# The first pair's blocks go to the inverse and back by VectorE transpositions, with a new list of the first 640 steps

## The chip, the cores and the metric

One core of one Trainium2 chip runs the whole kernel. The metric is the device time of one execution in microseconds (us), lower is better. A profile of one execution stands beside the timed runs: its span runs from the first instruction to the last, and the execution's own time is a little longer than that span.

The engines are named as in the profile: PE (TensorE), DVE (VectorE), ACT (ScalarE), POOL (GpSimd), and SP, which here does nothing but issue DMAs. "SPq" and "ACTq" are the time that a queue takes to issue a DMA.

## The reference

Two blocks follow each other. The first is a delta rule over 768 tokens, for 4 batches and 8 heads of 48 features:

```python
k_n = k / (np.linalg.norm(k, axis=-1, keepdims=True) + 1e-06)
state = np.zeros((B, H, D, D), dtype=np.float32)
for t in range(S):
    kt, vt, bt = (k_n[:, :, t], v[:, :, t], beta[:, :, t, None])
    y[:, :, t] = np.einsum('bhd,bhde->bhe', q[:, :, t], state)
    v_old = np.einsum('bhde,bhd->bhe', state, kt)
    state = state + bt[:, :, :, None] * np.einsum('bhd,bhe->bhde', kt, vt - v_old)
```

Its output, as x of 3072 tokens by 384 features, goes through the second:

```python
a = x @ w1          # 384 x 1024
b = x @ w2          # 384 x 1024
h = a * b @ w3      # 1024 x 1024
return (h @ w_out).astype(np.float32)   # 1024 x 384
```

q, k, v and beta come as float32. The four weights come as float64, so they are twice as many bytes, and the kernel makes float32 of them itself.

## The kernel before, in words

**The delta rule in chunks.** The 768 tokens are cut into 12 chunks of 64, and two chunks m = 2j, 2j+1 make a pair j. For each chunk a lower triangular system has to be inverted, of 64 x 64 for each of 32 heads (4 batches by 8 heads). It is done on blocks of 32 x 32: the two blocks on the diagonal of each system are inverted, and `corner` makes the third block out of them by matmuls. A pair has 2 chunks x 32 heads x 2 blocks = 128 diagonal blocks, one for each partition. `inverse(j)` (L483) holds one block in each partition, 32 x 32 = 1024 numbers in its free dimension, and eliminates them on DVE in 31 steps of two instructions (a product, L503, and a subtraction, L508).

**How the blocks come there and go back, before.** The scores `first_scores` or `scores` write U with tokens on the partitions. `to_blocks(m)` (L471) writes the blocks to a DRAM buffer Ud with 4 DMAs a chunk, `inverse` reads them back with one DMA (L489) into Ub, with blocks on the partitions. It ends with one DMA (L516) to a DRAM buffer Vd, and `from_blocks(m)` (L522) reads them with 4 DMAs a chunk into TT (L525) and 4 into T22 (L532), tokens on the partitions again. For the first two pairs the elimination runs in PSUM: ACT copies the unit matrix there (L497) and the result back to Vb (L512).

**The rest of a chunk.** `by_tensor` (L359) turns keys and queries to features on the partitions with PE, `squares` and `norms` make the scales of the keys, `corner` (L539) the inverse, `chain` (L606) the state, and `outputs` (L686) the transposed output xT. Since a matmul of the second block reads 128 partitions and a half has only 112 rows, `outputs` copies some rows of xT to free partitions by 6 DMAs a chunk (L748).

**The weights.** A piece of float64 is loaded by `piece` (L759) into one of 5 tiles named raw, which are used in turn, and made to float32 in three further steps: two ACT instructions, one of DVE (L776), one of POOL (L778). There are 36 pieces, P0 to P35: 8 of w_out, 16 of w3, 6 of w1, 6 of w2; a piece of w1 or w2 takes 4 DMAs, the others one. w3 is transposed on PE (`transpose_w3`, L828) and multiplied with w_out once (`fold`, L837: 8 folds of 8 matmuls), so that each token later goes through w3 @ w_out in one product.

**The second block.** `ab(u, jc, c0, c1)` (L851) makes a * b for 128 of the 1024 features and the tokens of a pair of chunks. For the first pair it is done for each chunk alone (256 tokens in a matmul, steps b0 to b7 and a00 to a07), for the next ones for both (512). `slab_sums`, `o` (L1067) and `result` make the output products with seven instead of eight block products (Strassen's scheme). The last pair takes `features` instead of `ab`.

**The order.** Nothing is scheduled when the kernel runs. ORDER is a list of 1379 step names that stands in the file; each name starts a generator or moves it to its next `yield`, and each engine and each DMA queue works off its own instructions strictly in that text order. So an instruction that waits holds up all behind it on its engine. Step names: k, q, v load a chunk; K, Q turn it; g, N are squares and norms; s and h are scores (in the first pair the keys' and the queries'), u writes blocks to DRAM, V is the inverse, e the corner, c the chain, y the outputs, P a piece, t and f the transposition of w3 and the fold, b and a the products of the second block, S, o, x its output, p and d the keys and queries by DMA and DVE from the fifth chunk on.

## Time and profile before

| | us |
|---|---|
| three timed runs | 575.88, 576.21, 573.61 (median 575.88) |
| the profiled execution | 575.02 |
| its span | 573.3 |
| PE busy | 537.3 (94%) |
| DVE busy | 336.7 (59%) |
| POOL busy | 173.1 (30%) |
| ACT busy | 143.6 (25%) |
| moved by DMA | 56.57 MB, mean 99 GB/s |

The page shows the busy share of each engine in 40 slices of 14.3 us each, then the chain of work that ended last, the costliest groups of instructions, and the DMA issues. The groups and the timeline count each float32 matmul twice, since PE runs it as two instructions: "x64" in a row of PE are 32 matmuls of the code. A row of the timeline gives the start, the duration, the engine, the line and the operation, the number of merged instructions, and in brackets the idle time ahead of it with what ended it. A row of the view by stretches gives, for each stretch, the busy time and the number of instructions of each engine, the granted PE clock (1.00 is full), the busy share of the DMA engines, and the rate in GB/s.

### The profile page before, as it was taken

Reading aid. Unit: us, or ns where it says so; the run is one execution under the profiler, and the core shown is the slowest. Engines: PE = TensorE matmul, PEld = TensorE weight load, DVE = VectorE, ACT = ScalarE, POOL = GpSimd, SP = SyncE. Lnnn points to the kernel's source line nnn. Section 1 sums busy time; section 2 is a strip of 40 time slices with the busy share of each in tenths; the row PEclk is TensorE's granted clock in tenths of the full one; section 3 lists DMA queues with packets and bytes.
Section 4 is the critical chain, followed back from the end, with each engine's and each line's share of the span. In section 5 each row is a group of like instructions: output and inputs, shape, how many; then the busy total and the mean of one; then the engine's idle time right before and its main releaser. Section 6 shows DMA issues by size and latency. Waiting matters only on the chain.

```text
span 573.3 us, 19695 instructions
## 1 busy us (share of the span) xinstructions
PE 537.3 (94%) x8588; PEld 393.3 (69%) x8588; DVE 336.7 (59%) x795; ACT 143.6 (25%) x289; POOL 173.1 (30%) x217
## 2 busy tenths in 40 slices
PE   2889888899999999998999999999999999989997
PEld 1765556688889744597644699444986446988897
DVE  4739823449854659765795735696264974123552
ACT  4466545624112110130120120110310102212210
POOL 6565543212883000524121332002731006610000
PEclk9979999999999999999999999999999999999999
DMA  9888997459746371564446425733325113010001
GB/s 218 233 242 229 216 198 148 90 128 173 126 74 111 61 137 32 110 98 84 92 75 110 63 47 105 125 65 82 42 46 125 20 51 58 18 53 5 0 1 55
DMA packets 202806, 56.57 MB, mean 99 GB/s; under 512 B 189952, under 2 KB 196096, under 8 KB 202720
## 3 DMA queue, kind: packets, MB, share of 16 engines
q1 hardware_dynamic: 200608, 54.92, 47.8%
q8 instruction: 67, 1.10, 0.8%
q10 hardware_dynamic: 2112, 0.39, 0.4%
q14 instruction: 19, 0.16, 0.1%
HBM read 43.09 MB, written 11.01 MB: 94 GB/s over the span
## 4 chain that ended last, share of the span: by engine, by line
PE 66%; DVE 11%; DMA 11%; SPq 4%; ACT 3%; issue 3%; POOL 2%; ACTq 0%; DVEq 0%; POOLq 0%
PE ps_f L858 26%; PE ps_f L1090 19%; PE ps_w L614 4%; PE ps_f L998 4%; DVE tb L503 4%; PE ps_w L719 4%; DMA raw<-in_moe_w_dram 4%; PE ps_w L998 2%; DVE ps_w L508 2%; PE ps_w L561 2%; DMA ktok<-in_k_dram 2%; DVE Vb L508 2%; DMA Vd<-Vb 2%; PE ps_w L437 1%; SPq L763 1%
## 5 line engine op out<-in xcount | busy, mean ns | idle before, releaser
L858 PE MATMUL ps_f<-xT,w2s 128*128 128x512 f32 (+1 forms) x288 | 107.1, 525 | 0.6 <-DVE ab L874 0.4
L858 PE MATMUL ps_f<-xT,w1s 128*128 128x512 f32 (+1 forms) x288 | 105.9, 524 | 0.3 <-DMA xT<-xT 0.3
L858 PEld LDWEIGHTS ps_f<-xT,w2s 128*128 128x128 f32 x288 | 53.9, 190 | 46.3 <-issue 41.3
L858 PEld LDWEIGHTS ps_f<-xT,w1s 128*128 128x128 f32 x288 | 54.1, 190 | 45.6 <-issue 42.5
L931 POOL TENSOR_TENSOR ab<-ab 128x256 f32<-128x256 f32 x80 | 56.0, 725 | 40.8 <-DVE ab L874 29.3
L1090 PE MATMUL ps_f<-w,ab 128*128 128x192 f32 x320 | 56.8, 331 | 2.0 <-DVE osb L1119 1.3
L1090 PEld LDWEIGHTS ps_f<-w,ab 128*128 128x128 f32 x320 | 51.6, 190 | 3.6 <-issue 2.8
L870 ACT COPY ab<-ps_f 128x512 f32<-128x512 f32 (+1 forms) x48 | 23.3, 515 | 121.5 <-PE ps_f L858 117.9
L503 DVE TENSOR_TENSOR tb<-Vb,Ub 128x31 f32<-128x31 f32 (+15 forms) x124 | 43.6, 352 | 15.8 <-DMA Ub<-Ud 12.1
L508 DVE TENSOR_TENSOR Vb<-Vb,tb 128x31 f32<-128x31 f32 (+15 forms) x124 | 45.1, 364 | 4.3
L837 PE MATMUL ps_f<-wo,w3T 128*128 128x384 f32 x128 | 44.9, 500 | 2.9 <-ACT w3T L831 1.9
L1090 PE MATMUL ps_f<-room,ab 128*128 128x192 f32 x240 | 43.2, 332 | 0.1
L299 POOL TENSOR_TENSOR sq<-ktok 128x384 f32<-128x384 f32 x24 | 20.3, 849 | 67.7 <-DMA ktok<-in_k_dram 39.0
L1090 PEld LDWEIGHTS ps_f<-room,ab 128*128 128x128 f32 x240 | 38.6, 190 | 1.2 <-issue 0.4
L837 PEld LDWEIGHTS ps_f<-wo,w3T 128*128 128x128 f32 x128 | 23.8, 194 | 18.6 <-ACT w3T L831 2.7
L874 DVE TENSOR_TENSOR ab<-ab,ps_f 128x512 f32<-128x512 f32 (+1 forms) x48 | 27.4, 589 | 13.3 <-PE ps_f L858 13.3
L600 POOL TENSOR_TENSOR vtok<-vtok,n 128x384 f32<-128x384 f32 x24 | 20.3, 850 | 45.3 <-DMA vtok<-in_v_dram 32.9
L577 ACT COPY T<-ps_w 32x512 f32<-32x512 f32 x24 | 13.8, 575 | 77.7 <-PE ps_w L561 67.2
L737 ACT COPY xT<-ps_w 112x256 f32<-112x256 f32 x48 | 14.3, 384 | 65.7 <-PE ps_w L719 65.7
L778 POOL TENSOR_TENSOR w<-w,raw 128x512 uint32<-128x512 uint32 x16 | 21.2, 1330 | 18.1 <-DVE w L776 14.3
L437 PE MATMUL ps_w<-KQ 48*64 48x128 f32 x320 | 21.8, 275 | 3.2 <-DVE PT L460 1.4
L503 DVE TENSOR_TENSOR tb<-ps_w,Ub 128x31 f32<-128x31 f32 (+15 forms) x62 | 21.0, 338 | 4.0 <-ACT ps_w L497 2.6
(148 smaller groups left out, 780.8 us busy)
## 6 DMA issues: line engine op xcount, KB each, us to landing
raw<-in_moe_w_dram SPq DMA_DIRECT2D x16, 512.0 KB, 5.6
vtok<-in_v_dram SPq DMA_DIRECT2D x24, 192.0 KB, 4.6
raw<-in_moe_w_dram SPq DMA_DIRECT2D x24, 192.0 KB, 5.0
out_dram<-osb SPq DMA_DIRECT2D x46, 96.0 KB, 1.8
ktok<-in_k_dram SPq DMA_DIRECT2D x44, 96.0 KB, 3.6
raw<-in_moe_w_out_dram SPq DMA_DIRECT2D x8, 384.0 KB, 5.1
Ud<-U SPq DMA_DIRECT2D x48, 64.0 KB, 2.0
Ub<-Ud SPq DMA_DIRECT2D x6, 512.0 KB, 3.9
```

What stands on the lines that cost most here:

```text
L437: pe.matmul(ps[half(z), 0, n : n + 128], lhsT=x[:, 0, :], rhs=x.rearrange("p j t -> p (j t)"), start=True, stop=True,)
L503: dve.tensor_tensor(out=tv, in0=V[:, 0 : s + 1, s : s + 1].to_broadcast([P, s + 1, n]), in1=U[:, s, s + 1 : BS].unsqueeze(1).to_broadcast( ...
L508: dve.tensor_tensor(out=o, in0=o, in1=tv, op=ALU.subtract)
L614: pe.matmul(out(ps, r, h, z), lhsT=lhs(r, h, z), rhs=rhs(r, h, z), start=True, stop=True,)
L719: i = pe.matmul(region(h, z, r), lhsT=lhs, rhs=rhs, start=part[n] not in part[:n], stop=part[n] not in part[n + 1 :],)
L837: pe.matmul(ps[:, 0:DM], lhsT=w3Ts[jc, kc // 4][:, kc % 4 * P : kc % 4 * P + P], rhs=wo(kc), start=(kc == 0), stop=(kc == KF - 1),)
L858: pe.matmul(ps[:].rearrange("p b c t -> p b (c t)"), lhsT=w[:, m, js], rhs=x[:, m, :, c0:c1].rearrange("p b c t -> p b (c t)"), start=(m = ...
L870: act.copy(out=t, in_=ps)
L874: dve.tensor_tensor(out=t, in0=t, in1=ps, op=ALU.mult)
L931: (dve if u == last else pool).tensor_tensor(out=o_, in0=x_, in1=y_, op=op)
L998: pe.matmul(ps[:, j, :], lhsT=w[j], rhs=x, start=first and j == 0, stop=j == 1, skip_group_check=not first,)
L1090: pe.matmul(ps[b][:, b, :], lhsT=ab_of(u, HF * f + i, t0), rhs=ws_[w][:, i], start=first and i == 0 and (b == 0 or n == "F"), stop=i == HF ...
```

## The change

Only the first pair (chunks 0 and 1, inverse 0) takes a new way; the other five pairs go through DRAM as before.

- **Into the inverse.** The two U tiles become one tile Upair, so that one DVE transposition reads both chunks. DVE transposes blocks of 32 x 32, so within each quarter of 32 partitions the (chunk, head) of a block becomes the partition, and token row and column lie in the free dimension. For that the block of the second token half has to lie in the columns of the first as well, so `keys_or_queries` makes the keys' scores with two matmuls of 32 rows each in place of one of 64 rows, and the second of them writes its block twice. `to_blocks` is not called for m = 0 and 1 (8 DMAs less), nor the load of Ub (1 less).
- **Out of the inverse.** Four transpositions, each of one quarter of 32 partitions and 1024 numbers, read the result in PSUM and write TT. The two ACT copies to Vb, the DMA to Vd, and 16 DMAs of `from_blocks` are not done. T22 is made by `from_engines`: 4 PE matmuls with the unit matrix and 2 ACT copies a chunk.
- **DMAs on the ACT queue.** Of the keys of chunks 0 and 1, two of four DMAs each are issued by ACT (before: all four of chunk 0 by ACT, all four of chunk 1 by SP). Of the 6 DMAs of xT of chunks 0 and 1, ACT issues 3.
- **More tiles for pieces.** 12 of the 36 pieces are loaded not into a raw tile but into kperm, qperm, or one of two parts of a tile of the KQ ring, all of which are unused at that time. kperm and qperm are no longer set to zero at the start.
- **The list.** The first 667 names of ORDER are replaced by 670 others; the last 712 are the same.

```diff
@@ ORDER
-k0 P12 beta P3 P3 g0 P8 g0 P8 P0 g0 P12 K0 K0 k1 P12 P13 P12 K1 K0 q1 P3 beta P0 g0 P0 P10 P8 g0
...
+k0 P12 g0 k1 K0 P2 P8 P12 beta K1 g0 P8 P13 g0 K0 P1 g0 g0 V0 P2 P8 P10 K1 P5 P2 K0 P12 g0 beta s0
...
+P26 t8 V0 f5 P27 P35 t6 t14 P20 t6 q2 V0 P24 k3 P15 P15 f4 V0 V0 h0 f4 v0 t15 f4 t7 e0 Q2 e0 P20
+e0 t7 e0 Q2 P20 P21 f3 e0 K2 g1 e1 e0 g1 v1 q3 P27 f3 n0 P26 P32 P24 e0 P20 e1 P35 K1 P21 e1 e1
+P28 K2 n0 P35 c0 Q2 P24 f7 c0 e1 P28 g1 f7 g1 e1 P27 P21 P27 P33 K2 P21 f3 f7 c0 c0 K0 P29 e1 t12
+P25 t13 P32 n1 c1 t13 t12 K3 g1 P29 K3 K3 y0 P34 k4 g1 y0 f6 Q3 y0 P29 n1 c1 P33 P29 y0 c1 P24 c1
+P33 f6 y1 P34 b5 Q3 P25 Q3 N1 y1 f6 s3 P34 P25 P31 s2 s3 P30 s2 y1 b4 P31 y1 P30 s3 s3 b5 s3 P34
+P33 b6 P25 b2 u3 s2 s2 a07 P30 s2 b4 b6 P32 b3 a07 u2 V1 P31 s3 v2 P30 b4 g2 b2 b5 a07 V1 s2 V1 b3
+b0 b4 g2 b6 a07 n2 b5 V1 P31 a04 b0 a00 V1 v3 a06 b6 g2 V1 c1 a04 a00 b1 V1 V1 a01 V1 b1 V1 V1 a06
+T V1 V1 V1 a02 b7 V1 P32 T a01 V1 a02 V1 a03 n3 a03 V1 V1 p4 b7 V1 a04 T V1 Q3 n3 V1 a00 a01 V1 V1
+a05 a04 n2 V1 a05 a00 V1 V1 a01 p4 a03 V1 b0 a03 a02 k5 b1 b2 V1 V1 V1 b0 V1 V1 S0 V1 g2 a02 b3 d4
+b1 V1 g2 T V1 g2 b3 b2 b7 V1 d4 a05 a05 g2 a06 c1 b7 g2 o0 S0 g2 c2 a06 e2 S0 S0 e2 x0 e2 c2 e3 N1
+o0 e2 e2 d4 S0 e2 V2 S0 p5 g2 o0 c2 e3 d4 Q0 S0 p5 x0 N1 S0 c2 e3 x0 o0 e3 S0 e3 c2 e3 N2 c2 S0 c3
+S0 S0 S0 o0 c3 x0 y2 y2 v4 d5 c3 o0 n4 c3 y3 d5 v5 s4 S0 d5 y3 d5 x0 S0 x0 s4 s4 x0 s5 S0 y3 s4 x0
...
@@ load_crossed
-                dma(
+                dmas[z](
@@ keys_or_queries
+                    if j:
+                        pe.matmul(
+                            ps[half(z ^ h % 2), h % 2, n : n + C],
+                            lhsT=x[:, 0, :], rhs=x[:, 1, :], start=True, stop=True,
+                        )
+                        continue
+                    own = x[:, 0, BS:C].unsqueeze(1).to_broadcast([D, 2, BS])
+                    for y, rhs in enumerate((x[:, 0, :], own)):
+                        pe.matmul(
+                            ps[quarter(2 * z + y), h % 2, n : n + C],
+                            lhsT=x[:, 0, BS * y : BS * y + BS], rhs=rhs, start=True, stop=True,
+                        )
@@ inverse
-        sync.dma_start(out=U[:], in_=Uds.pop(j)[:])
+        if j == 0:
+            dve.transpose(
+                out=U[:].rearrange("p s t -> p t s"),
+                in_=Upair[:, :, 0 : NR * H * C].rearrange("p m (g t) -> p t m g", t=C)[:, 0:BS],
+            )
+        else:
+            sync.dma_start(out=U[:], in_=Uds.pop(j)[:])
...
+        if j == 0:
+            for x in range(4):
+                dve.transpose(
+                    out=TTpair[quarter(x), :, :, :, quarter(x % 2)].rearrange(
+                        "s m r h t -> s t m (r h)"
+                    ),
+                    in_=V[quarter(x)].rearrange("p s t -> p t s"),
+                )
+                if x == 3:
+                    held.clear()
+                yield
+            return
@@ from_blocks
+    def from_engines(m):
+        TT, T22, n = TTs[m], T22s[m], NR * H // 2 * BS
+        ps = two_banks()
+        for z in range(2):
+            x = quarter(2 * z + 1)
+            for e in range(2):
+                pe.matmul(
+                    ps[quarter(2 * (z ^ e)), e, 0:n], lhsT=ident[x, x],
+                    rhs=TT[x, :, :, BS:C].rearrange("s r (a e) t -> s e (r a) t", e=2)[:, e],
+                    start=True, stop=True,
+                )
+        yield
+        for z in range(2):
+            x = quarter(2 * z)
+            act.copy(
+                out=T22[x].rearrange("s r (a e) t -> s e (r a) t", e=2),
+                in_=ps[x, :, 0:n].rearrange("s e (g t) -> s e g t", t=BS),
+            )
+        yield
     def from_blocks(m):
+        if m < 2:
+            yield from from_engines(m)
+            return
@@ outputs
+                dma = act.dma_start if u == 0 and e else sync.dma_start
@@ piece
+    GUESTS = {10: "k", 2: "0", 9: "q", 18: "1", 19: "k", 11: "q", 14: "0", 15: "1", 26: "k", 21: "q", 32: "k", 34: "q"}
+    spare = in_turn(work, [P, B, NP, 2, C], "KQ", 3, "spare")
...
+        if i in GUESTS:
+            raw = guest(GUESTS[i])
+        else:
+            raw = in_turn(ffn, [P, CW, 2], "raw", 5, "raw", U32)
@@ load_k
+        other = act if m < 2 else sync
+        ktoks[m] = load_crossed(k, m, (other.dma_start, sync.dma_start), "ktok", 4)
```

131 lines of the change are left out of this document (63 added, 68 removed).

## The prediction

> **What bounds the kernel now.** I read the page first, then four stretches, then the timeline of each engine in the stretch that is not full. On the page, the first line is PE's busy share in tenths, the second PE's granted clock, the third the share of the DMA engines.
>
> ```profile
> PE   2889888899999999998999999999999999989997
> ...
> PEclk9979999999999999999999999999999999999999
> DMA  9888997459746371564446425733325113010001
> ```
>
> PE is full from about the eighth slice on. Before that it isn't, and there the DMA engines are nearly full. The borders of the stretches are starts on PE: 37.0 the first fold of w3 (L837), 114.7 the first product of the second block (L858), 196.8 the first product of the second pair.
>
> ```profile
> 0.00:37.00 37.00, 21.58 (x548) 19.30 (x548) 20.60 (x46) 16.24 (x30) 22.42 (x35) 0.93 0.87 204
> 37.00:114.70 77.70, 68.26 (x1288) 45.82 (x1284) 43.12 (x119) 47.50 (x92) 31.70 (x30) 0.99 0.82 193
> 114.70:196.80 82.10, 81.10 (x1457) 71.76 (x1453) 54.65 (x138) 19.87 (x46) 36.19 (x43) 1.00 0.68 113
> 196.80:573.30 376.50, 366.37 (x5306) 256.44 (x5304) 218.33 (x494) 59.95 (x122) 82.83 (x110) 1.00 0.35 66
> ```
>
> PE idles 15.4 us before 37, 9.4 from there to 114.7, 1.0 in the third stretch, 10.1 in the last. The last stretch has the same names in the same order after the change. So a gain can only come from the first fold starting sooner and from the 9.4 us; behind 114.7 every added PE instruction and every new wait costs its full length. What the second stretch waits for stands in DVE, the queues and the chain:
>
> ```profile
> 27.34 5.54 SPq L477 DMA_DIRECT2D Ud<-U  x8
> 36.25 0.42 SPq L763 DMA_DIRECT2D raw<-in_moe_w_out_dram  x1
> 37.02 6.23 PE L837 MATMUL ps_f<-wo,w3T 128*128 128x384 f32 x16
> 41.74 0.19 DVE L503 TENSOR_TENSOR tb<-ps_w,Ub 128x31 f32<-128x31 f32 x1 [0.93 <-ACT ps_w L497]
> 68.61 0.20 DVE L508 TENSOR_TENSOR ps_w<-ps_w,tb 128x31 f32<-128x31 f32 x1
> 69.94 5.09 DMA Vd<-Vb
> 75.09 1.92 SPq L525 DMA_DIRECT2D TT<-Vd  x4
> 77.06 4.08 SPq L532 DMA_DIRECT2D T<-Vd  x4
> 79.87 0.71 DVE L544 STREAM_TRANSPOSE T<-TT 128x512 f32<-128x512 f32 x1 [7.90 <-DMA TT<-Vd]
> 88.33 3.11 SPq L525 DMA_DIRECT2D TT<-Vd  x4
> 91.48 1.98 SPq L532 DMA_DIRECT2D T<-Vd  x4
> 104.18 11.32 SPq L748 DMA_DIRECT2D xT<-xT  x12
> 108.02 1.64 DMA xT<-xT
> 114.74 2.86 PE L858 MATMUL ps_f<-xT,w1s 128*128 128x256 f32 x12
> ```
>
> The first inverse runs on DVE from 41.74 to 68.81. Its result goes out through DRAM for 5.1 us, comes back, and DVE sits idle 7.9 us until 79.87. The outputs of chunk 0 then wait for SP, which issues weight pieces until 104.18; xT lands at 109.7, and the second block starts.
>
> **The change, term by term, on the profiled execution (575.02 us; the median of the three runs is 575.88, so 0.9 above it).**
>
> *Start of the folds.* A fold needs all eight pieces of w_out. Before, the last of them is SP's 36th DMA, at 36.25, behind 8.62 MB of its queue; in the new list it is the 22nd, behind 6.65 MB. With ACT's 0.39 MB, SP moved 9.0 MB by 36.7 us, 0.246 MB/us, so the 22nd is through its queue near 29. But the last piece's DVE step now stands behind the first seven steps of the inverse, and its POOL step behind that. I put the first fold at 33.0, 4.0 sooner; bounds 29 (queue alone) and 37 (no gain). Before it, 32 more score matmuls a chunk (64 in all; 64 records of that line took 1.99) cost 4 us in a stretch that has 15.4 idle.
>
> ```profile
> 17.94 1.99 PE L395 MATMUL ps_w<-KQ 48*64 48x64 f32 x64
> 82.46 0.76 PE L561 MATMUL ps_w<-T,U 33*33 33x32 f32 x64
> 93.76 1.11 PE L367 MATMUL ps_f<-ident,ktok 64*48 64x64 f32 x64
> 117.52 0.33 PE L437 MATMUL ps_w<-KQ 48*64 48x128 f32 x2
> 118.69 5.45 PE L858 MATMUL ps_f<-xT,w1s 128*128 128x256 f32 x24
> L837 PE MATMUL ps_f<-wo,w3T 128*128 128x384 f32 x128 | 44.9, 500 | 2.9 <-ACT w3T L831 1.9 <-POOL wo L778 1.0
> L828 PE MATMUL ps_f<-ident,w 128*128 128x128 f32 x44 | 6.1, 275 | 0.2 <-POOL w L778 0.2
> ```
>
> *PE's work from the first fold to the first L858.* 68.3 before. Three quarters of the scores of chunks 2 and 3 move behind it: the last quarter took from 117.52 to 118.69, so 3 x 1.17 = 3.5 less. 32 more transposing matmuls (x64) come from ahead of it, +1.1, and 32 first-queries scores, +1.9. T22 costs 8 matmuls of 256 columns: singly 16 records x 0.224 (5.37 to the next start, over 24) = 3.6; but the corner's 33x32 matmuls of two row groups take 22 ns each, under half of what 32 columns would at that rate, so 1.8. Sum 69.6.
>
> *The first inverse.* Out go 8 DMAs of Ud (5.5 us of SP), the load of Ub, and 4 us between. SP begins to write U at 27.34, so U is ready about there, and I leave it so; the transposition follows. ACT's two copies stand behind a w_out piece that goes through SP's queue near 27 by the rate above and has to land: the first step at 32.5, not 41.74. The steps:
>
> ```profile
> 127.70 0.19 DVE L503 TENSOR_TENSOR tb<-ps_w,Ub 128x31 f32<-128x31 f32 x1 [1.68 <-ACT ps_w L497]
> 153.16 0.20 DVE L508 TENSOR_TENSOR ps_w<-ps_w,tb 128x31 f32<-128x31 f32 x1
> ...
> L353 DVE STREAM_TRANSPOSE KQ<-kperm 128x512 f32<-128x512 f32 x16 | 11.1, 697 | 0.7 <-PE ps_w L719 0.7
> L778 POOL TENSOR_TENSOR w<-w,raw 128x512 uint32<-128x512 uint32 x16 | 21.2, 1330 | 18.1 <-DVE w L776 14.3
> ```
>
> The second inverse lasts 25.7 with twelve foreign DVE instructions of some 0.33 between its steps, so 21.7 alone. Between the new first one's steps stand eleven pieces' shifts and five others, 6.8 in all: it ends at 61.0. The four transpositions of 1024 columns are shown by no row. From below: the same operation takes 0.70 for 512 columns, so 1.39 for twice that, less one instruction's fixed part of at most 0.16 (31 columns take 0.19): 1.24. From above: no engine here is slower per column than POOL's 1330 ns for 512, so 2.66. I take 1.24, the row of the same operation: with two shifts between them TT is complete at 66.7. PE reaches T22 at 33 + 5/8 of 44.9 (28.1) + 36 x 0.137 (4.9) + 1.1 + 1.9 + 0.2 = 69.2. So the inverse, which was waited for, now has 2.5 us in hand, and what the removed DMAs cost (Vd, 16 reads) is saved only down to PE's own work. If the cover goes, each further us is a us of the total.
>
> [...]
>
> *What stays of the 9.4 us.*
>
> ```profile
> 45.34 4.78 PE L837 MATMUL ps_f<-wo,w3T 128*128 128x384 f32 x14 [1.01 <-POOL wo L778]
> 67.55 2.85 PE L837 MATMUL ps_f<-wo,w3T 128*128 128x384 f32 x8 [1.90 <-ACT w3T L831]
> ```
>
> Waits for pieces like these two, 2.9, should go, since 12 pieces no longer wait for a raw tile. The other 6.5 are in part waits between dependent matmuls of corner, chain and outputs, which the new list has too; I keep 3.5 (bounds 1 and 9). xT is hidden: between chunk 0's outputs and the first L858 the list has some 10 us of other PE work, SP has 17.3 us less to issue ahead of it (the Ud, Ub, Vd, TT and T rows above), and three of the six DMAs go by ACT. There each costs under 0.94 us (SP's row for twelve), and the first copies of the second block's products stand behind chunk 1's three; four PSUM banks let PE go on for four products, 5.4 us, so I cost that at nothing, and without the banks at 2.8. First L858 at 33.0 + 69.6 + 3.5 = 106.1, 8.6 sooner.
>
> *Behind it.* The scores moved here, +3.5. In chunk 3's chain one product now follows chunk 2's last with no other matmul between, and ahead of the state that it needs DVE does 15 instructions of norms, 0.19 or more each: +1.8, an estimate between 1 and 4. Scores that wait for a PSUM bank: +0.5. Against 1.0 idle before: 81.1 + 3.5 + 2.3 = 86.9 for 82.1, 4.8 later.
>
> *Sum.* 575.02 - 8.6 + 4.8 = 571.2. Against the median that is -0.8%; about 0.5%, or 2.9 us, is what a measurement of this kernel can tell from no change.
>
> **The rivals.**
>
> *The transpositions are slow.* At 2.66 each the four take 10.6, TT is complete at 72.4, T22 waits 3.2: 574.4, no change. For: they move single numbers with steps of 128 and 256 bytes. [...]
>
> *The gain is larger.* First fold at 30.5 and only 1.5 of waits: 571.2 - 4.5 = 566.7. For: SP's queue loses 26 DMAs, 17.3 us, while the DMA engines are 82% busy in that stretch. Against: pieces still pass through DVE behind the inverse.
>
> *The folds start no sooner.* The pieces still come one behind the other through ACT, DVE and POOL: start at 37, and 575.2.
>
> *The second inverse becomes the wait (slower).*
>
> ```profile
> 115.90 5.64 SPq L477 DMA_DIRECT2D Ud<-U  x8
> 123.21 0.34 SPq L489 DMA_DIRECT2D Ub<-Ud  x1
> 154.55 0.35 SPq L516 DMA_DIRECT2D Vd<-Vb  x1
> 161.85 0.76 PE L561 MATMUL ps_w<-T,U 33*33 33x32 f32 x64
> ```
>
> Before, Ud of the second pair is issued 1.2 us after the first L858; the corner that needs the result stands 40.3 us after the last of these DMAs and PE came to it 47.1 after its first L858, just as it was ready. Now the scores and the norms they need come after the first L858, so I put the last Ud issue 10 us after it, the corner's data at 50.3; PE arrives after 43.0 of products, 4.7 scores, 2.2 chain and 3.0 others, at 52.9. So 2.6 us are in hand. From there each us costs one; it ends slower than before by over 2.9 when Ud is 9.3 us later than I put it, at about 580. For: norms, outputs of chunk 1, three xT DMAs and eight weight DMAs stand ahead in the queues. Against: all of those are in place before 10 us by the durations above.
>
> **How the numbers follow.** Forecast (571.2, its own range 568 to 574): 0.46. Transpositions slow: 0.19. Larger gain: 0.12. No sooner start: 0.10. Second inverse: 0.13. Faster by over 0.5% (below 573.0): four fifths of the first and all of the third, 0.49, plus a little of the second: 0.51. Slower by over 0.5% (above 578.8): most of the last, and some 0.1 where several terms miss in one direction: 0.22. Within: 0.27. The range runs from the larger gain with its bounds (F at 29, 1 us of waits: 564) to the slower case, 580.
>
> **What the new profile would show.** Right: first L837 near 33, first inverse step near 32.5, four transpositions of about 1.24 that end near 67, no DMA between the first inverse and T22, first L858 at 104 to 108, first L858 of the second pair at 191 to 195, the last stretch at 376.5 as before. Wrong, if the first L837 is at 37 or the transpositions take over 2 us, if L858 starts past 110, or if PE idles more than 4 us between its first L858 and the second pair's, above all in front of the second pair's corner.

## The result: slower by 1.6%, and the profile after

The changed kernel took 584.38 us in the median of its runs (583.02 to 585.03), the kernel before 575.58 beside it (573.61 to 576.21). The ratio is 1.0156, with a 95% interval of 1.0125 to 1.0187. The forecast was 571.2, in a range of 564 to 580: it missed the sign and the range. In later runs on three chips the same kernel lay lower, at 1.0025 to 1.0056 (below). A ratio leaves out runs that lie over 1.5% above the fastest of the same kernel (five of the changed kernel's 34 later runs, one of the 89 of the kernel before beside all later ones), while a median counts all. So two things are to be explained: why the gain of 4 us came in none of them, and why the time moves so much.

Of the page of the profiled execution of the changed kernel (584.46 us, span 582.7): PE's busy share in 40 slices, PE's granted clock, the share of the DMA engines, and the queue that brings instructions (packets, MB, share).

```profile
PE   3699898999999899998899999999989999999997
...
PEclk9999979999999799998999999999989999999999
DMA  8997975464455271464246425734213303010001
...
q8 instruction: 68, 1.11, 0.8%
```

From the third slice to the eighth PE is fuller than before (9 9 8 9 8 9 for 8 9 8 8 8 8). But the clock has notches in the 6th, 14th, 19th and 30th slice, where the page of before has none; it has one in the third. The four stretches, with the borders that the prediction used (first fold, first product of the second block, first product of the second pair); columns are PE, PEld, DVE, ACT and POOL busy, PE clock, DMA share, GB/s:

```profile
0.00:35.63 35.63, 20.07 (x549) 17.27 (x549) 22.66 (x55) 20.49 (x39) 20.15 (x31) 1.00 1.00 255
35.63:109.61 73.98, 70.03 (x1289) 46.57 (x1285) 49.23 (x114) 45.44 (x84) 33.40 (x30) 0.95 0.75 170
109.61:200.63 91.02, 87.57 (x1599) 77.23 (x1593) 55.84 (x139) 19.53 (x47) 35.43 (x42) 0.96 0.50 89
200.63:582.70 382.07, 369.52 (x5312) 259.87 (x5308) 218.30 (x494) 60.23 (x122) 82.47 (x110) 0.99 0.34 64
```

The second block starts 5.1 us sooner than before, which is a part of the forecast gain. Then 8.9 us are lost in the third stretch, of which 4.8 were forecast, and 5.6 in the last, where not a name of the list has changed. Most of what was not forecast is in the next rows. Timeline of the changed kernel: start, duration, engine, line, operation, and in brackets the idle time ahead with what ended it.

```profile
33.02 0.19 DVE L523 TENSOR_TENSOR tb<-ps_w,Ub 128x31 f32<-128x31 f32 x1 [1.16 <-ACT ps_w L517]
63.46 0.20 DVE L528 TENSOR_TENSOR ps_w<-ps_w,tb 128x31 f32<-128x31 f32 x1
...
72.22 1.07 PE L562 MATMUL ps_w<-TT,ident 32*32 32x256 f32 x8 [1.72 <-DVE TT L532]
73.23 1.96 PE L368 MATMUL ps_f<-ident,X 64*48 64x64 f32 x64
...
76.02 4.29 PE L911 MATMUL ps_f<-wo,w3T 128*128 128x384 f32 x8
...
80.23 1.11 PE L368 MATMUL ps_f<-ident,ktok 64*48 64x64 f32 x64
...
98.45 0.21 PE L368 MATMUL ps_f<-ident,ktok 64*48 64x64 f32 x1 [1.38 <-issue]
...
176.45 1.15 PE L671 MATMUL ps_w<-S,KQ 48*64 48x48 f32 x64 [1.22 <-DVE S L737]
...
191.74 0.38 PE L456 MATMUL ps_w<-KQ 48*64 48x64 f32 x2 [1.09 <-issue]
...
269.91 4.55 PE L1164 MATMUL ps_f<-room,ab 128*128 128x192 f32 x16
...
279.63 2.87 PE L1164 MATMUL ps_f<-room,ab 128*128 128x192 f32 x16
...
429.44 0.33 PE L671 MATMUL ps_w<-R,TT 64*64 64x48 f32 x6 [1.72 <-issue]
```

Three things are to be seen. T22 waits 1.72 us for the transpositions, where the prediction had 2.5 in hand. PE stops for 1.1 to 1.7 us at several places with "issue": it waits for nothing that the profile shows. And the same work takes two lengths: 64 records of transposing matmuls 1.96 or 1.11, sixteen of output products 4.55 or 2.87. The windows of PE say where the longer ones come from (columns: PE busy, PE clock, DMA share, GB/s):

```profile
65.31:68.72 3.41, 3.41 (x12) 1.00 1.00 182
68.72:72.13 3.41, 1.35 (x7) 1.00 0.96 158
72.13:75.55 3.42, 3.33 (x113) 0.50 1.04 214
75.55:78.96 3.41, 3.41 (x45) 0.50 1.34 180
78.96:82.37 3.41, 3.41 (x137) 1.00 0.92 189
188.19:191.60 3.41, 2.03 (x87) 1.00 0.24 69
191.60:195.01 3.41, 3.27 (x89) 0.50 0.21 46
427.12:430.53 3.41, 1.69 (x49) 1.00 0.00 0
430.53:433.94 3.41, 3.41 (x13) 0.50 0.02 5
```

In this profile the granted clock is 1.00 or 0.50 for entire windows of 3.41 us, which follow each other on a fixed grid: it is half from 72.13 to 78.96, 191.60 to 198.42, 270.10 to 273.52 and 430.53 to 433.94. Where PE was busy for only 1.35 us of a window (in front of T22), the next two ran at half clock; the stops at 191.74 and 429.44 had the same effect. The window in front of T22 is low in each of the four profiles of the changed kernel (1.35, 1.47, 0.81 and 1.34 busy), with one or two halved windows behind it.

### The profile page after: what moved, and what is told of

The parts are those of the page before. It is cut to its first block, busy times and chain, and to the rows that moved or that the text cites. A ratio compares the mean times of both kernels' runs of the same rounds, so it can differ in the third digit from the quotient of the medians.

```text
span 582.7 us, 19957 instructions
## 1 busy us (share of the span) xinstructions
PE 547.2 (94%) x8732; PEld 400.9 (69%) x8732; DVE 346.0 (59%) x800; ACT 145.7 (25%) x291; POOL 171.4 (29%) x213
## 3 DMA queue, kind: packets, MB, share of 16 engines
q8 instruction: 68, 1.11, 0.8%
## 4 chain that ended last, share of the span: by engine, by line
PE 84%; DMA 4%; DVE 4%; issue 3%; ACT 2%; SPq 1%; POOL 0%; ACTq 0%; DVEq 0%; POOLq 0%
PE ps_f L932 36%; PE ps_f L1164 20%; PE ps_w L671 5%; PE ps_f L1072 4%; PE ps_w L776 4%; PE ps_f L911 4%; PE ps_w L618 3%; PE ps_w L1072 2%; PE ps_w L456 2%; PE ps_w L450 2%; DMA raw<-in_moe_w_out_dram 2%; DVE TT L532 1%; PE ps_f L902 1%; DMA ktok<-in_k_dram 1%; PE ps_f L368 1%
## 5 line engine op out<-in xcount | busy, mean ns | idle before, releaser
L932 PE MATMUL ps_f<-xT,w1s 128*128 128x512 f32 (+1 forms) x288 | 107.2, 524 | 0.6 <-POOL w2s L851 0.5
L1164 PE MATMUL ps_f<-w,ab 128*128 128x192 f32 x320 | 58.4, 337 | 2.0 <-DVE osb L1193 1.3
L1164 PEld LDWEIGHTS ps_f<-w,ab 128*128 128x128 f32 x320 | 53.2, 195 | 3.7 <-issue 2.8
L911 PE MATMUL ps_f<-wo,w3T 128*128 128x384 f32 x128 | 46.6, 516 | 0.2 <-issue 0.2
L1164 PE MATMUL ps_f<-room,ab 128*128 128x192 f32 x240 | 46.3, 350 | 0.0
L1164 PEld LDWEIGHTS ps_f<-room,ab 128*128 128x128 f32 x240 | 42.0, 203 | 0.9
L462 DVE TENSOR_TENSOR U<-ps_w,wt 128x512 f32<-128x512 f32 x20 | 13.7, 689 | 21.3 <-PE ps_w L456 21.3
L456 PE MATMUL ps_w<-KQ 48*64 48x64 f32 x640 | 23.8, 229 | 2.5 <-issue 2.5
L1193 DVE TENSOR_TENSOR room<-room,ps_f 128x384 f32<-128x384 f32 (+1 forms) x13 | 7.0, 537 | 30.9 <-PE ps_f L1164 30.9
```

The lines of the kernel that those rows point to most:

```text
L456: pe.matmul(ps[half(z ^ j), 1, n + C * j : n + C * j + C], lhsT=x[:, 0, :], rhs=x[:, j, :], start=True, stop=True,)
L911: pe.matmul(ps[:, 0:DM], lhsT=w3Ts[jc, kc // 4][:, kc % 4 * P : kc % 4 * P + P], rhs=wo(kc), start=(kc == 0), stop=(kc == KF - 1),)
L932: pe.matmul(ps[:].rearrange("p b c t -> p b (c t)"), lhsT=w[:, m, js], rhs=x[:, m, :, c0:c1].rearrange("p b c t -> p b (c t)"), start=(m = ...
L1164: pe.matmul(ps[b][:, b, :], lhsT=ab_of(u, HF * f + i, t0), rhs=ws_[w][:, i], start=first and i == 0 and (b == 0 or n == "F"), stop=i == HF ...
```

## The experiments

The theory formed from these rows has two parts. **Stops:** PE runs dry at the border of an instruction block, when the block is not there in time. Counting PE's records from 0 (matmuls, weight loads, its own waits), every "issue" stop of 0.2 us or more in the profiles of this study, 136 in 17 profiles, lies at place 193 or 194 of a group of 256. The queue q8 brings 68 packets with 1.11 MB, that is 16 KB each, and PE has 17,586 records, or 68.7 groups; before it had 17,299. The packets' times in the traces bear this out: if the borders are numbered from record 449 on, the nth packet of q8 ends 1.2 to 1.8 us before PE goes on at the nth border in all 136 stops, and at the 1,003 borders without such a stop PE never crosses sooner than 1.2 us after it. The 32 added matmuls of scores a chunk are 256 records in all, a whole block; T22's eight matmuls are 32. So the borders behind T22 fall 32 records elsewhere in the same work. In no profile do two packets start less than 3.27 us apart, while 64 matmul records with their 64 loads, half a group, can be done in 1.1, or 2.2 a group: several groups of such work in a row outrun the packets. **Half clock:** a window in which PE idles too much halves the clock of the next (1.35, 2.03 and 1.69 us busy of 3.41 in the rows above).

The rival was that the queues and DMAs, which the change moves, hold PE up: other pieces land late and the stop only shows as "issue".

Since a place alone shows no cause, the experiments move the borders and leave the queues, or the reverse. Rows by stretch have the columns PE busy, PE clock, DMA share, GB/s from here on; a ratio is to the kernel before on the same chip, in brackets its 95% interval.

### One part of the change alone

List, tiles, queues and doubled score matmuls of the changed kernel, but the blocks go through DRAM as before, and T22 comes from there. The list gets u1 u0 behind the first pair's scores and loses one V0, one e0 and one e1, which have nothing left to do; the first V1 moves behind the first inverse:

```diff
@@ inverse
-        if j == 0:
-            dve.transpose(
...
-        else:
-            sync.dma_start(out=U[:], in_=Uds.pop(j)[:])
+        sync.dma_start(out=U[:], in_=Uds.pop(j)[:])
...
-        if j == 0:
-            for x in range(4):
...
@@ from_blocks
...
-        if m < 2:
-            yield from from_engines(m)
-            return
```

> The new list and the further tiles for pieces, but the first pair goes through DRAM as before (eight writes of Ud, the load of Ub, Vd, sixteen reads; no T22 matmuls; the steps of the list that only the new path has are dropped, and the second pair's first memset moves behind the first inverse, whose tile it needs). By the prediction's steps: folds begin as in after, near 35.6, but the inverse's result comes by DMA some 9 to 11 us behind the inverse's end (about 65), so PE, which reaches that place near 70, waits 4 to 9 us; first product of the second block at 113 to 118, third stretch 86 to 88, last stretch 376.5 (the 8 matmuls less put the block borders back where they stood before): total 578 to 584, more if a half-clock window follows the wait. Rival: the transpositions matter little and the list alone carries the change: within 2 us of after.

It took 592.17 us, a ratio of 1.0313 (1.0256 to 1.0371). Its view by stretches (PE alone; the second and the last), and two rows of its timeline, where DVE and PE wait:

```profile
31.51:123.34 91.83, 72.79 (x1274) 0.87 0.77 174
...
211.96:588.46 376.50, 366.00 (x5311) 1.00 0.35 66
```

```profile
83.86 0.71 DVE L580 STREAM_TRANSPOSE T<-TT 128x512 f32<-128x512 f32 x1 [13.12 <-DMA TT<-Vd]
84.63 1.13 PE L597 MATMUL ps_w<-T,U 33*33 33x32 f32 x64 [6.74 <-DVE T L580]
```

DVE sits 13.12 us in front of the blocks that come back through DRAM and PE 6.74, and of the second stretch 23.9 us are at half clock (its mean is 0.87). It is 16 to 18 longer than with the engines' way, by the four profiles of the changed kernel. So in this list the engines' way does what the prediction said of it: the trip through DRAM is gone. The last stretch is 376.5, as before, although list, tiles and queues are the new ones: here T22's 32 records are missing.

The reverse, the engines' way with the list, tiles and queues of before; the list loses u0 and u1 and gets one V0, one e0 and one e1 more. In this kernel T22's products overwrite a part of chunk 0's query products before they are read, so that half the batches of chunk 0 come out with other numbers; the work is the same.

```diff
@@ ORDER
-P2 Q1 P9 P10 P1 P2 t4 h1 t4 q0 P18 P10 t0 P2 Q0 u1 P9 t5 Q0 Q0 P1 P18 u0 P1 P6 h1 t1 P6 P4 t2 P7
+P2 Q1 P9 P10 P1 P2 t4 h1 t4 q0 P18 P10 t0 P2 Q0 P9 t5 Q0 Q0 P1 P18 P1 P6 h1 t1 P6 P4 t2 P7 P18
...
@@ inverse
-        sync.dma_start(out=U[:], in_=Uds.pop(j)[:])
+        if j == 0:
+            dve.transpose(
...
+            for x in range(4):
+                dve.transpose(
...
@@ from_blocks
+        if m < 2:
+            yield from from_engines(m)
+            return
```

> The old list, the old buffers for pieces and the old queues for k and xT, with the first pair's blocks by transpositions and T22 by matmuls. By the prediction's steps: no Ud and Ub DMAs, first inverse from about 38 instead of 41.7, its end near 65, four transpositions of 1.9 us, T22 near 74 where the corner began at 81 before; PE had only 9.4 us idle there, so the first product of the second block comes 3 to 5 sooner, 110 to 112; third stretch 82 to 84. Theory A (instruction blocks): T22's 8 matmuls move the borders by 32, so the last stretch is 378 to 382 instead of 376.5. Total 574 to 579. Rival: the transpositions are waited for as the DMAs were, with a half-clock window behind them: first product at 114 or later, total 578 to 584.

It took 582.05, a ratio of 1.0122 (1.005 to 1.0193). Its last three stretches:

```profile
37.96:118.02 80.06, 70.67 (x1307) 0.96 0.66 158
118.02:199.76 81.74, 80.87 (x1456) 1.00 0.68 113
199.76:577.98 378.22, 367.71 (x5308) 1.00 0.34 65
```

The second stretch is 2 to 3 longer than before, not shorter, with 1.7 us of wait for TT in front of T22 and 6.8 at half clock; the last is 1.7 longer. In the old list, taking the trip through DRAM away shortens nothing. Neither part alone gains anything.

### Moving the borders alone

Some of the matmuls that turn the keys of chunk 0 (and 1) are done twice, into the same place. One more matmul is four records of PE; nothing else in the kernel changes. The three kernels have one of these lines each: the kernel before with 8 more (32 records), the changed kernel with 32 more (128), and with 56 more (224).

```diff
+    AGAIN = {0: 8}
+    AGAIN = {0: 32}
+    AGAIN = {0: 32, 1: 24}
...
-                    pe.matmul(
+                    for _ in range(2 if i == 0 and NR * H * z + H * r + h < AGAIN.get(m, 0) else 1):
+                        pe.matmul(
```

The kernel before with 32 records more, whose borders then lie behind the first pair as those of the changed kernel do:

> The kernel before, and 8 of the transposing matmuls of the keys of chunk 0 issued twice: 32 more PE instructions, 0.3 us of work in a stretch that waits for DMA. Theory A (instruction blocks): the borders in the last 376 us stand where they stand in after, so that stretch takes about 382 instead of 376.5, with stops of about 1.4, 0.9 and 1.7 and one or two half-clock windows behind them; total 578 to 582. Rival B (what pieces and queues do): no change, 573 to 576.

It took 581.48 in the median of ten runs, a ratio of 1.0074 (1.0028 to 1.0121); the profiled run is the second longest of them (584.70). Eight such matmuls at the rate of 64 records in 1.1 us are 0.3 us of work, and they lie ahead of the folds, where PE idles. Its last three stretches, a row of its timeline, and the same work in the kernel before:

```profile
37.13:118.72 81.59, 72.46 (x1292) 0.93 0.76 183
118.72:203.06 84.34, 82.25 (x1454) 0.99 0.62 110
203.06:582.97 379.91, 367.67 (x5309) 0.99 0.34 65
```

```profile
429.99 0.33 PE L617 MATMUL ps_w<-R,TT 64*64 64x48 f32 x7 [1.76 <-issue]
```

```profile
420.32 1.10 PE L614 MATMUL ps_w<-R,TT 64*64 64x48 f32 x64
```

The stop of 1.76 us is in the same group of matmuls as the one of 1.72 in the changed kernel, one record apart (ahead of the last 7 and the last 6 of 64), and in the kernel before there is none there. With no other list, tile or queue the last stretch is 3.4 longer than in the profile of before; the two stretches ahead of it are longer too, by 3.9 and 2.2.

The changed kernel with 224 records more, which with its own 288 make 512, two whole blocks; and with 128 more:

> The kernel after, and 56 of the 64 transposing matmuls of the keys of chunks 0 and 1 issued twice (same values, 224 more PE instructions, in the stretch that waits for DMA anyway). Theory A, instruction blocks: PE's instructions arrive in packets of 16 KB, 256 instructions each; after stands still seven times, 9.1 us in all, with nothing to wait for, each time at instruction 193 or 194 of a block. The change adds 288 PE instructions, which moves every border behind it by 32; 224 more make it 512, so the borders in the last 380 us stand where they stood before. A expects the stretch from the second pair's first product to the end back at about 376.5 us (382.0 in after), with one stop of 0.7 instead of 1.4, 0.9 and 1.7, the half-clock windows of that stretch gone, the stop of 1.1 at 191.7 with its two half-clock windows gone too, and a total of 574 to 577. Rival B, what the pieces and queues do (other tiles, other DMA order) makes the end slower: 382 there again and a total of 583 to 586.

> The kernel after, and all 32 transposing matmuls of the keys of chunk 0 issued twice: 128 more PE instructions, so the borders behind them stand 128 from where they stood in after. Theory A: stops with nothing to wait for are again all at instruction 193 or 194 of 256, at other work than in after; total anywhere from 575 to 588, and what it differs from after, taken from the first fold on, is the difference in stops and in half of the half-clock time, within 3 us. Rival B (the time is set by other things): 583 to 586, stops at the same work as in after.

The last stretch of the one and of the other:

```profile
207.51:584.82 377.31, 366.40 (x5312) 1.00 0.35 66
```

```profile
200.01:584.52 384.51, 369.01 (x5312) 1.00 0.34 64
```

The first row is the last stretch with 224 more: 377.3, so it is near the length of before again. With 128 more (the second row) it is 384.5, with 6.8 us of stops in it. As a whole both are slower (585.81, 1.0185 from 1.0128 to 1.0241; and 587.68, 1.0227 from 1.0175 to 1.028): with 224 more, 8.1 us of stops fall ahead of the folds, where matmuls of keys and scores stand close together, and 3.95 and 3.31 in the next two stretches. Over all profiles of the study the last stretch sorts by its borders:

```text
borders as before (mod 256)  376.1 376.5 376.5 376.5 377.3 377.9
moved by 32                  377.7 377.7 377.9 378.2 378.4 379.0 379.4 379.9 380.3 382.1
moved by 160                 384.5
```

The groups nearly part; the 377.9 of the first lies in the second. The rival falls for this stretch: new queues with old borders give 376.1 to 377.9, old queues with new borders 378.2 and 379.9. Less its stops and half of its time at half clock, the last stretch is 374.2 to 376.7 in all 17 profiles. That PE waits for its block is read from the place of the stops and the landing of the packets; no record shows when PE asks for one.

### What is in front of T22

The window ahead of T22 was to be filled, so that the clock stays whole: 56 matmuls of constants, into the banks that T22 takes (224 records, so the borders behind are those of before, and the last stretch is 376.1).

```diff
+        if m == 0:
+            for x in range(56):
+                pe.matmul(
+                    ps[quarter(x % 2 * 2), x % 2, 0:C], lhsT=ident[quarter(1), quarter(1)],
+                    rhs=ident[quarter(1), 0:C], start=True, stop=True,
+                )
```

> The kernel after, with 56 matmuls of constants (224 instructions) put between the last transposed weight and T22, into the bank that T22 then overwrites: PE is busy for most of the 1.7 us in which it waited for the inverse. Theories A and C together: borders behind it as before the change, and no half-clock windows from 72 to 79, so the first product of the second block 3 to 4 us sooner than in after (near 106) and a total of 570 to 575, below the run with the 56 early ones by 2 to 4. If the clock does not follow PE's work, the two windows stay and the total is within 1 us of the run with the 56 early ones.

```profile
70.27 5.79 PE L561 MATMUL ps_w<-ident 32*32 32x64 f32 x110 [1.69 <-DVE TT L532]
```

From its timeline. A miss, 589.3 us, 1.0256 (1.0197 to 1.0314): the filler itself waited 1.69 us, since its banks are still held until the transpositions have read the inverse from PSUM, and then it ran at half clock (the mean of its stretch, 32.03 to 116.19, is 0.92). It filled nothing, and stands as work on the path.

Instead, the 32 transposing matmuls of chunk 2's queries (64 records), which need nothing of the inverse, go ahead of T22:

```diff
-f4 t7 e0 Q2 e0 P20
+f4 t7 Q2 e0 e0 P20
```

> The kernel after with one step of the list moved: the query transposes of chunk 2 (64 matmuls, 1.1 us) stand in front of the T22 matmuls instead of behind them. Theory C (a window with less than about 1.7 us of PE work is followed by half clock): the wait of 1.7 us in front of T22 shrinks to about 0.6, the window around it holds over 2.1 us of work, the one or two half-clock windows behind it (68 to 79) are gone; first product of the second block 2 to 4 us sooner than in the unchanged kernel of the same chip, total 2 to 5 lower. Rival: PE only waits 1.1 later, at the corner that needs the same result, and the half clock follows there: within 1 us of the unchanged kernel.

The last three stretches, and two rows of the timeline:

```profile
33.84:105.46 71.62, 66.12 (x1292) 1.00 0.74 177
105.46:191.15 85.69, 83.85 (x1599) 1.00 0.51 89
191.15:571.40 380.25, 368.02 (x5313) 0.99 0.34 65
```

```profile
68.47 1.11 PE L368 MATMUL ps_f<-ident,X 64*48 64x64 f32 x64
70.31 0.63 PE L562 MATMUL ps_w<-TT,ident 32*32 32x256 f32 x8 [0.73 <-DVE TT L532]
```

In this profile the wait at T22 is 0.73, and no window from the first fold to the second pair is at half clock. The two stretches then last 71.6 and 85.7, somewhat less than the 73.1 and 86.9 of the prediction. But this is the fastest of twelve runs (573.12), and even it has 380.25 in the last stretch, with 2.7 of stops; the median was 577.25, a ratio of 1.0039 (1.0011 to 1.0068). On another chip:

> The kernel after with the query transposes of chunk 2 in front of T22, again. Theory C: no half-clock window at 68 to 79, from the first fold to the first product of the second block about 72 us where the unchanged kernel takes 74 to 76, total 2 to 4 below after_fourth. If later stops give the gain back: that stretch shorter, the total within 1 us of after_fourth.

575.96, 1.0006 (0.9975 to 1.0037), and its profile does have two halved windows, from 68.0 to 74.9. They follow a wait of 2.20 us for a piece in front of w3's last transposition, which left 1.21 us of work in its window; for T22 itself PE does not wait there. So the move takes the wait at T22 away, and another wait can still empty a window. That it helps is open: in the same two batches the changed kernel took 576.96 and 578.97.

T22 by DMA from tile to tile in place of its matmuls and copies, so that the borders are those of before (the list loses one e0 and one e1):

```diff
-                pe.matmul(
-                    ps[quarter(2 * (z ^ e)), e, 0:n], lhsT=ident[x, x],
...
+                sync.dma_start(
+                    out=T22[quarter(2 * (z ^ e))].rearrange("s r (a e) t -> s e (r a) t", e=2)[:, e],
+                    in_=TT[quarter(2 * z + 1), :, :, BS:C].rearrange(
...
-            act.copy(
```

> The kernel after, with T22 filled by four DMAs from tile to tile for each of chunks 0 and 1 instead of four matmuls and two ScalarE copies. That takes 8 matmuls (32 PE instructions) out, so the borders of the instruction blocks behind them stand where they stood before the change, and PE no longer waits at T22, since T22 is used 9 us later. Theories A and C: no low window and no half clock at 68 to 79; first product of the second block 2 to 5 sooner than in the unchanged kernel (103 to 106); last stretch 376 to 377.5 without the stop of 1.7 near 425; third stretch as it is; total 569 to 574, 4 to 9 below the unchanged kernel on the same chip. Rival: SP's queue stands at these DMAs until the transpositions are done and the pieces behind them come late: first product at 109 or later, no gain.

Two rows of its timeline:

```profile
68.62 0.66 PE L895 MATMUL ps_f<-ident,w 128*128 128x128 f32 x4 [2.21 <-POOL w L844]
...
72.42 0.79 PE L611 MATMUL ps_w<-T,U 33*33 33x32 f32 x40 [1.89 <-DVE T L594]
```

A miss too: 580.94, 1.0103 (1.0069 to 1.0136). The wait for the inverse only moved from T22 to the corner (1.89), and 13.7 us of the second stretch were at half clock. The last stretch was 377.9.

### How long the transpositions are

The four transpositions with straight order on both sides, so the inverse's numbers do not come where they belong and the output is not the reference's; all the rest is the same work.

```diff
-                        "s m r h t -> s t m (r h)"
+                        "s m r h t -> s m (r h) t"
...
-                    in_=V[quarter(x)].rearrange("p s t -> p t s"),
+                    in_=V[quarter(x)],
```

> The kernel after, with the four transpositions of the inverse reading and writing runs of 32 numbers instead of hopping at each number; this leaves out the right arrangement of the inverse, the work around it is the same. If the hops make the transposition slow: about 1.24 us each instead of 1.9, the wait of 1.7 in front of T22 gone, and, if the granted clock falls after a window of little PE work (theory C), also the two half-clock windows from 72.1 to 79.0 gone: first product of the second block near 105, total 578 to 581 with the end of after unchanged. If reading PSUM or the four-byte size is what costs, 1.9 again and 583 to 586. If the clock falls for another reason, the product comes 1.7 sooner and no more, total near 582.5.

The rows of the tile view (minimum, median and maximum in ns; first and last start), of the changed kernel and of this one:

```profile
L532 DVE STREAM_TRANSPOSE TT<-ps_w x4: 1899/1944/1967, 63.9 to 70.3; 32x1024 f32<-32x1024 f32 x4
```

```profile
L532 DVE STREAM_TRANSPOSE TT<-ps_w x4: 1230/1245/1255, 63.9 to 68.2; 32x1024 f32<-32x1024 f32 x4
```

The estimate of 1.24 was exact for straight order, 1.245; the steps of 128 and 256 bytes cost 0.70 more each. T22 then waited 0.37 in place of 1.72, and neither profile of this version has a halved window right behind T22, where all four of the changed kernel have one or two; other halved windows, behind stops, remain in both. The times were 577.49 (1.0023, from 0.9985 to 1.006), and beside the changed kernel on one chip:

> The kernel after with the four transpositions in straight order, as before in this study (it leaves out the right arrangement of the inverse), now beside the unchanged kernel on one chip. Each transposition 1.25 us; T22 begins 2 to 2.7 sooner than in the unchanged kernel, no low window in front of it. If that wait and its half clock cost what theory C says, total 3 to 5 below the unchanged kernel; if the time comes back as a wait further on, within 1.5.

575.17 (0.9995, from 0.9966 to 1.0024) against 576.96 of the changed kernel there: 1.8 us less, with intervals that overlap.

### The kernels again

The changed kernel once more, on three chips, and the kernel before on one of them:

> The kernel after, unchanged, on another chip. If stops and half-clock windows sit where the program puts them: 583 to 586, clock 0.977 to 0.982, stops at the same seven borders. If their length depends on what the DMA engines do at that moment: the same borders, other lengths, other half-clock windows, and a spread of 5 us or more between runs.

> The kernel after, unchanged, once more. Theory A and C (stops at block borders whose length depends on the moment, half-clock windows after a window with less than about 1.7 us of PE work): stops again at instruction 193 or 194 of 256 at the same work as in the two earlier profiles, a low window in front of T22 with one or two half-clock windows behind it, and runs spread over 573 to 586. What is open is the level: 584 as in the result on record, or 577 as in the second look.

> The kernel after, unchanged, once more. If the level of 584 is a matter of the chip or the hour: either level can come. If it was chance over runs: median 575 to 579 again, with single runs to 585. In either case a last stretch of 377.5 to 382 with the stop of 1.7 to 2.0 at the same instruction near 420 to 430, and one or two half-clock windows behind T22's wait.

> The kernel before, unchanged, with a profile of its own. Theory A: its stops lie at instruction 193 or 194 of 256 and at the same work as in the first profile (2.7 us in all then); from the first fold on 1.5 to 4 us of stops and under 4 us of half clock, a last stretch of 376 to 378, total 573 to 577. If the account of the first profile was luck: stops and half clock as in the changed kernel, 6 us or more from the first fold on, at the same total.

The changed kernel took 577.18 (1.003, from 0.9994 to 1.0066), 576.96 (1.0025, from 1.0 to 1.005) and 578.97 (1.0056, from 1.0021 to 1.0092); its 34 runs there spread from 572.3 to 584.9. The kernel before took 574.7 (0.9981, from 0.9953 to 1.0009). The stretches of the first of these three profiles:

```profile
33.26:107.13 73.87, 69.39 (x1288) 46.33 (x1284) 51.53 (x116) 46.08 (x85) 33.38 (x30) 0.95 0.74 173
107.13:194.57 87.44, 84.21 (x1600) 74.18 (x1593) 55.77 (x139) 19.52 (x47) 35.49 (x42) 1.00 0.52 90
194.57:572.28 377.71, 366.10 (x5312) 256.54 (x5308) 218.02 (x494) 60.27 (x122) 82.78 (x110) 1.00 0.34 65
```

The same program, 10.4 us shorter than the profile above: 3.6 in the third stretch and 4.4 in the last, where this one has 2.57 of stops for 3.99 and no halved window for two. So the 584 of the result is the upper end of what this program does, and why its runs there lay so near to each other is open. The ratios of the later runs are a loss of 0.25 to 0.56%, with intervals that begin at 0.9994, 1.0 and 1.0021; by the medians of all runs it is 0.4 to 0.7%.

An account over the four profiles of the changed kernel and two of the kernel before, means in us. Stops are counted in full, half clock at half its time; both are ceilings, since the halved work measured above ran 1.5 to 1.8 times as long, and a stop can lie beside another wait.

```text
stretch             difference   stops   half clock / 2   rest   predicted
to the first fold         -3.1       -                -   -3.1        -4.0
second                    -2.7    +0.7             +1.8   -5.3        -4.6
third                     +7.8    +1.8             +1.3   +4.7        +4.8
last                      +2.7    +1.9             +0.8    0.0         0.0
sum                       +4.7    +4.4             +3.9   -3.6        -3.8
```

That the sum of the rest comes so near the prediction is chance, given the ceilings. What it says is that PE's work and the waits with a name moved by about what was forecast, stretch by stretch, and that the two costs without a name are large enough to have taken all of it.

## Why the prediction was wrong

**The sum's frame failed.** Its step was "The last stretch has the same names in the same order after the change", and so "the last stretch at 376.5 as before", and for the rest PE's work plus waits for named things. The same names do not make the same time: the stops at instruction blocks cost 1.8 to 1.9 more in the third and last stretch each. In the last they moved with the 32 records of T22, and the border experiments show this without the change itself. In the third they come with the new order of the work: the new list has 2.15 us of them with the old borders too (list_only), the old list none with T22's 32 records (transpositions_only). Of the 1,139 crossings in the 17 profiles 136 cost 0.2 us or more, one of them 2.76 in front of 48x48 products (after_56_at_T22), where small float32 matmuls stand close. The profile of before had such stops too (0.67 and 0.50 us in front of chunk outputs, 2.7 in all), and the prediction counted them among "waits between dependent matmuls" without asking what they were.

**The price of a wait failed too.** "If the cover goes, each further us is a us of the total" was too little. The wait of 1.72 us in front of T22, with 0.44 for a piece shortly before, left a window with 1.35 us of work, and 6.8 us at half clock followed. Work there ran 1.5 times as long (the fold of eight, 4.29 for 2.85) to 1.8 (1.96 for 1.11), so the wait drew some 2 to 3 us behind it; in the other three profiles one halved window followed, about half of that. A window did not have to be empty for half clock to follow: of windows at whole clock from 42 us on, in all profiles of the study, all 16 with under 1.5 us of work were followed by half clock, 20 of 42 with 1.5 to 2.06, and 2 of 2,527 above.

**The four transpositions were mis-sized,** at 1.24 for 1.94. The row it was scaled from has other strides: in straight order these four took 1.245 each (after_TT_straight), with the steps of 128 and 256 bytes 1.94, or 1.9 ns a column. The rival of slow transpositions therefore came true in mechanism, with a wait of 1.7 for its 3.2.

**The other steps held.**

```text
                                   predicted        after    the three later profiles
first fold                         33.0 (29-37)     35.63    33.26  33.47  32.50
first step of the inverse          32.5             33.02    31.30  31.54  31.44
end of the inverse                 61.0             63.66    62.15  62.16  62.06
TT complete                        66.7             72.2     70.7   70.6   70.5
PE's work in the second stretch    69.6             70.0     69.4   69.2   68.0
first product, second block        106.1 (104-108)  109.61   107.13 109.51 107.51
PE's work in the third stretch     84.6             87.6     84.2   84.5   86.2
first product, second pair         191-195          200.63   194.57 197.80 198.42
```

The inverse lasted 30.6 us for 28.5, and with the transpositions that makes TT 5.5 later than forecast, while PE came 1.3 later. The stall in chunk 3's chain was 1.22 for 1.8. The two waits in front of folds (2.9 in the rows of before, which "should go") are gone. But PE now waits for a piece in front of w3's transpositions, 0.4 in two profiles of the changed kernel and 2.2 and 2.5 in the other two: this step held only in part. A slip without weight: the last piece of w_out is SP's 37th DMA before and its 23rd after, where the prediction has 36th and 22nd. xT did not hold the second block up. The rival of the second inverse did not come: at the corner of the second pair PE waits for the inverse in no profile of the changed kernel. That the folds start no sooner is excluded by all four.

Of the signs that the prediction named for its own failure none is in the result's profile: transpositions under 2 us, the second block ahead of 110, PE idle for 3.45 us (under 4) in the third stretch, no wait at the second corner. The loss went by all of them, since they looked only for waits with a name.

## What to carry to other kernels

Where PE's instructions are many and small, the profile's "issue" rows in front of a matmul are to be counted, and an edit that adds or drops PE instructions can move all of them behind it: here 32 records more took the last stretch from 376.5 us to 379.9 (before_8_more), and 224 more took it from 382.1 to 377.3 (after_56_more), so price such an edit with some us in either direction, even for stretches that it does not touch. A wait on PE is to be priced with the clock: here all 16 windows of 3.41 us with under 1.5 us of work were followed by half clock, and the wait in front of T22 drew one or two such windows behind it. The DMA trip that lay beside other work was worth nothing here without the new list: taken away alone, it gave 1.0122.

## What the runs showed of the hardware that was not expected

Eight repeated matmuls, 0.3 us of work where PE idles, made the kernel before slower by 0.74% (0.28 to 1.21); what they change for the rest of the kernel is the place of the instruction blocks. Packets of 256 PE instructions started at least 3.27 us apart in all 17 profiles, and in none of them did PE enter a block sooner than 1.19 us after its packet had ended. The same program on one core took 572.3 to 584.9 us, and what differs between two of its profiles is mainly stops and halved windows. A DVE transposition in 32 x 32 blocks of 1024 float32 columns from PSUM took 1.245 us in straight order (after_TT_straight) and 1.94 where both sides hop (the changed kernel).

None of the versions beats the kernel before. The changed kernel without the pieces in borrowed tiles wasn't tried, so their share of the sooner start is open.
